# Softmax sums from chunks added on VectorE, split pairs by query halves, and TensorE's order as one script

## The chip, the cores and the metric

The kernel runs on one core of a Trainium2 chip. The metric is device microseconds of one execution. Before the change the median of three runs is 417.61 us (417.56 to 417.89). Besides, one execution was taken with the hardware profiler; views of that profile and its trace are what the text argues from. The engines are TensorE (PE, its weight loads PEld), VectorE (DVE), ScalarE (ACT), GpSimd (POOL) and SyncE (SP, which here only issues DMAs).

## The reference

Cosine attention over 8 batches of 12 heads, 448 tokens, head size 64, followed by a two-matrix layer with x * cos(x) between:

```
q_n = q / (norm(q) + 1e-06);  k_n = k / (norm(k) + 1e-06)
attn = softmax(q_n @ k_n.T / 0.1)            # over the keys
x = (attn @ v) as [3584, 768]                # 12 heads of 64 side by side
h = x @ w_in                                 # 768 -> 2048
out = (h * cos(h)) @ w_out                   # 2048 -> 768, float32
```

What matters for the change is the denominator of the softmax: for each query the sum over 448 keys of the exponentials.

## The kernel before

**Work.** Two heads make a pair; there are 48 pairs (g), three to a unit (u, 16 units), six to a batch. The 448 tokens are seven blocks of 64. Keys lie on partitions, so for a pair the exponentials are a half chunk PH (one block of keys: its two halves of queries on the two halves of the partitions, 448 columns for both heads) and three full chunks PX 1 to 3 (two key blocks on 128 partitions each; 448 queries for each of two heads, 896 columns, bf16). `scores` (L722) writes the four chunks: a matmul group of four 64x64 tiles, 224 columns for the half chunk (L740) and 448 for a full one (L732), and then an exponential on ACT (L747).

`attend` (L752) makes from them the value product and the sums, in one of four PSUM tiles of two banks each (AV, SC0, SC1, MP): bank 0 holds the product (64 dimensions of two heads on 128 partitions), bank 1 the sums. Its stages 0 and 1 take the half chunk (`rest` L763, or `row` L777 for the product alone), stage 2 the three full chunks (`av` L784, four tiles of 128 rows by 32 columns), with the sums behind it as matmuls whose weights are ones. For these there are several forms:

- Pairs whose sums go through a DMA ("not direct", 34 of 48). `sm` (L791) puts chunks 1 and 2 into rows of their own, four matmuls of 448 columns. In units 6 to 15 ("alone", 28 pairs) `sm2` (L807) follows with the half chunk and chunk 3 in matmuls of 224, 336 and 112 columns; in pairs 6 and 12 to 16 `sm1` (L799) with chunk 3 in four of 224, while the half chunk's sums come from `rest`. Product and sums are then copied out together, 128x896 floats, by DVE (L889) or, for even pairs after 18 that are not in "vector", by ACT (L886). `chain` (L923), once a unit: gather the sums by DMA into 128 partitions (three transfers, two in units 2 and 4), add the parts (L938), reciprocal (L941), write to DRAM (L942), broadcast back (L944), and POOL multiplies x = product * reciprocal (L948).
- "Direct" pairs 0 to 5 and 47: sums by `sm32` (L827, strided groups of 224) or `sm64` (L842), Ln and Exp(-x) on ACT (L896 to L912).
- "Quarters" or split pairs 7 to 11, 17 and 23, also direct: in `quarter` (L817) the key blocks on the two halves of the partitions go to different banks, value product of one beside the sums of the other, in two rounds of three groups of 448 columns (L823), with `rest` of two groups of 224 (L773) between. ACT takes the Ln over 448 sums (L910), then the Exp (L912); DVE copies the product (L915); POOL multiplies (L916).

After the six pairs of a batch, `m1` (L963) computes h: 96 matmuls of 128x128 by 448 columns (L956), ACT the sine (L985), DVE the product into gT (L987). The second matrix M2 is worked off in small steps between the pieces of attention: `m2_quarters` (L1036) makes steps of four 64x64 matmuls of 384 columns (L1054); an output tile takes 32 steps and both banks of MP, and is copied out by DVE (L1021).

**Order.** Each operation is entered with what it reads and writes. PE's order is the order of entry (from the first M1 on); `Program.play` sorts the other engines' operations by a model with due times, and waits are set from the dependencies. An operation with `lock=True` (all of POOL's, and few of DVE's) shares one slot with the others of that kind in this model. PE's order comes from `pair` (L1227) with shares of M2 from "grid", "given", "lead" and others in PLAN, and for pairs 19 to 22 and 25 to 46 from a written "script" that `play` (L1185) reads: `s19.1` is scores chunk 1 of pair 19, `a`, `b`, `c` are the stages of `attend`, `f4` is four steps of M2, `m3` is M1 of batch 3. The PSUM tile of each piece is chosen in turn (`touch` L1188).

**Beside it.** SP issues the loads of q and k, the transposes of later pairs (L698), gathers, broadcasts and outputs. POOL squares (L643) and scales (L681) q and k for later units, and issues the loads of v; DVE reduces the squares (L650).

Of the kernel before, what the change touches and what calls it, by code (L numbers as in the profile page):

```python
# [18 lines left out]
    "swapped": {},  # L19
    "early": {2: (3, 3), 4: (3, 3), 5: (3, 3), 6: (3, 3)},  # L20
    "vector": (32, 38),
    "alone": range(6, 16),
    "script": {19: """
        s19.0 f9 s19.1 s19.2 f9 s19.3 f3 a18 f4 b18 s20.0 c18 c19 s20.1 f2 a19 f2 b19 s20.2 f4 s20.3 f4 s21.0 a20 f4 s21.1 b20
        f4 s21.2 f6 s21.3 f6 o201 c20 m2 c21 a21 f4 s22.0 b21 f7 s22.1 f5 s22.2 s22.3 f11
        """, 25: """
        a24 s25.0 f3 s25.1 f2 b24 c24 s25.2 f4 s25.3 f5 s26.0 f3 s26.1 f4 s26.2 f3 s26.3 a25 f3 b25 s27.0 c25 c26 s27.1 f1 a26
        f2 b26 s27.2 f4 s27.3 f3 m3 c27 a27 f4 b27 s28.0 f4 s28.1 f4 s28.2 f4 s28.3 s29.0 f3 s29.1 f3 s29.2 f6 s29.3 f2 a28 f2
        b28 s30.0 c28 c29 s30.1 a29 f3 b29 f1 s30.2 f2 s30.3 f4 s31.0 f6 s31.1 s31.2 f5 s31.3 f7 a30 f4 b30 s32.0 c30 c31
        s32.1 f2 a31 f2 b31 s32.2 f7 s32.3 f5 s33.0 s33.1 f5 s33.2 f5 s33.3 f6 m4 c32 c33 a32 f4 b32 a33 f4 b33 s34.0 f8 s34.1  # L30
        f4 s34.2 s34.3 f2 s35.0 f4 a34 f4 b34 f2 s35.1 c34 s35.2 f5 s35.3 f11 s36.0 s36.1 f5 a35 f5 b35 s36.2 f6 c35 s36.3 f5
        s37.0 f5 s37.1 f6 s37.2 s37.3 f10 a36 f3 b36 f3 s38.0 c36 c37 s38.1 a37 f4 b37 s38.2 f4 s38.3 f8 s39.0 s39.1 a38 f4
        b38 f4 s39.2 f4 s39.3 f4 c38 m5 c39 a39 f4 b39 s40.0 f4 s40.1 f4 s40.2 f4 s40.3 s41.0 f5 s41.1 f4 s41.2 f5 s41.3 a40
        f2 b40 s42.0 c40 c41 s42.1 a41 f3 b41 f1 s42.2 f4 s42.3 f8 s43.0 s43.1 f4 s43.2 f3 s43.3 f7 a42 f2 b42 s44.0 c42 c43
        s44.1 f2 a43 f2 b43 s44.2 f9 s44.3 f3 s45.0 s45.1 f3 s45.2 f3 s45.3 f10 m6 c44 c45 a44 f4 b44 a45 f4 b45 s46.0 f8
        s46.1 f1 s46.2 f6 s46.3 f5
        """},
    "after": (0, 1, 2, 0, 1, 2, 0, 1),
# [5 lines left out]
    "last": ((0,), (1,), (2,)),  # L44
    "folded": (0, 1, 2, 3),
    "grid": {2: (16, 5, 6), 3: (11, 3, 4), 4: (8, 2, 3)},
# [4 lines left out]
    "second": 0,  # L51
# [5 lines left out]
    "mixed": (3, (3, 0, 1, 2, 0, 1, 2, 0), (2, 3, 4, 0, 1, 5)),  # L57
# [7 lines left out]
    "six": (0, 8, 4, 4),  # L65
    "cycle": {13: 3, 14: 3, 15: 3, 16: 3, 17: 3, 18: 3, 46: 3, 47: 3},
    "quarters": (7, 8, 9, 10, 11, 17, 23),
    "turns": {3: (3, 0, 1, 2, 0, 1, 2, 0)},
    "lastbank": 2,
    "end": (4, 3, 0),  # L70
    "parts": {3: (0, 1, 2, 3), 4: (0, 1, 3), 14: (0, 1, 3), 10: (0, 1, 3)},
# [5 lines left out]
    "given": {13: (0, 0, 3, 2), 16: (4, 0, 5, 2), 22:(1,2,5,6), 34: (12, 4, 5, 6), 46: (12, 4, 3, 4), 47: (2, 2, 5, 4)},  # L77
    "roots": (3, (14, 0), (10, 0)),
    "lead": {33: 5, 45: 6, 12: 13, 21: 13},
    "vloads": {3: [(4, "x6"), (5, "x6")], 4: [(6, "x11")], 5: [], 6: [(7, "x15"), (8, "x15")]},  # L80
    "behind": {2: 8, 3: 0, 4: 8},
    "direct": (0, 1, 2, 3, 4, 5, 7, 8, 9, 10, 11, 17, 23, 47),
}
# [335 lines left out]
def bass_cosine_attention__then__act_gcu_kernel(  # L419
# [28 lines left out]
    XS = [UP * S * (3 + i) + HQ * (i + 1) for i in range(2)]  # L448
    XW = XS[1] + UP * S
# [36 lines left out]
    sums = sbs("sums", 2, [128, 3 * SPR], F32)  # L486
# [6 lines left out]
    tail = sb("tail", [128, 32], BF16)  # L493
# [21 lines left out]
    xsv = [xu.ap()[:, x : x + UP * S].rearrange("p (g s) -> p g s", g=UP) for x in XS]  # L515
# [9 lines left out]
    TURN = (1, 2, 0, 1, 2, 0, 1, 0)  # L525
    AFTER = PLAN["after"]
# [5 lines left out]
    SH = S * 3 // 4  # L532
# [51 lines left out]
    for x in XS:  # L584
        dve(lambda e, x=x: e.memset(xu.ap()[:, x - HQ : x], 0.0), (), ["gap"], HQ)
    dve(lambda e: e.memset(tail.ap(), 0.0), (), ["tail"], 32)
    for n in range(2):
        dve(lambda e, n=n: e.memset(tail.ap()[BP * n : BP * n + BP, 16 * n : 16 * n + 16], 1.0), ["tail"], ["tail"], 16)
# [133 lines left out]
    def scores(g, c, bank=None):  # L722
        j, y = g % 2, g % NT
        name, ph = PHs[1 + (c + 1) % 2 if bank is None else bank]
# [11 lines left out]
        def half(e):  # L736
# [11 lines left out]
            keys, [("PX", j, c) if c else ("PH", g % 3)], 2 * n, "E", label="exp%d.%d" % (g, c))  # L748

    opened, held, turned = {}, {}, set(PLAN["swapped"])  # L750

    def attend(g, direct, stages=(0, 1, 2)):  # L752
# [6 lines left out]
        ws = slice(32, 96) if direct else slice(64, 128)  # L759

        folded, swapped, alone = g in PLAN["folded"], g in turned, not direct and u in PLAN["alone"]

# [541 lines left out]
    for g in range(TD, LT):  # L1304
        transposes(g)
# [85 lines left out]
```

## Time and profile before

| what | value |
|---|---|
| median of three runs | 417.61 us |
| span of the profiled execution, first to last instruction | 415.5 us; median less span 2.1 us |
| busy: PE, ACT, POOL, DVE | 406.5, 269.1, 242.9, 192.1 us |
| exponentials on ACT, 128x896 (L747) | 144, mean 918 to 923 ns |
| evacuation 128x896 on DVE (L889), on ACT (L886) | 22 of 1.09 us, 12 of 0.92 us |
| POOL: scale (L681), square (L643) | 48 and 44, mean 1.68 and 1.69 us |
| Ln of 448 sums (L910), of 224 (L896) | 0.54 us, 0.36 us |
| DVE copies of 448 columns (L915), of 384 (L1021) | 0.62 us, 0.55 us |

The span is what the profiler saw between the first and the last instruction; the time of a run is longer by what lies around it. "Busy" counts an engine's instructions; on PE the ends of overlapping matmuls are modelled, and so the time between the starts of two groups says more of a group's cost than its length.

### The profile page before, as it was taken

Reading aid. Unit: us, or ns where it says so; the run is one execution under the profiler, and the core shown is the slowest. Engines: PE = TensorE matmul, PEld = TensorE weight load, DVE = VectorE, ACT = ScalarE, POOL = GpSimd, SP = SyncE. Lnnn points to the kernel's source line nnn. Section 1 sums busy time; section 2 is a strip of 40 time slices with the busy share of each in tenths; the row PEclk is TensorE's granted clock in tenths of the full one; section 3 lists DMA queues with packets and bytes.
Section 4 is the critical chain, followed back from the end, with each engine's and each line's share of the span. In section 5 each row is a group of like instructions: output and inputs, shape, how many; then the busy total and the mean of one; then the engine's idle time right before and its main releaser. Section 6 shows DMA issues by size and latency. Waiting matters only on the chain.

```text
span 415.5 us, 13462 instructions
## 1 busy us (share of the span) xinstructions
PE 406.5 (98%) x6018; PEld 241.3 (58%) x6018; DVE 192.1 (46%) x257; ACT 269.1 (65%) x361; POOL 242.9 (58%) x193
## 2 busy tenths in 40 slices
PE   7799999999999999999999999999999999999997
PEld 3454556655556655665566556675566656655565
DVE  4564744455663257323753087321962254223421
ACT  4987578984888746977498567674588656603500
POOL 4999977889772575948964577536896200150000
PEclk9999999999999999999999999999999999999999
DMA  8999999979979997779955991989964900441023
GB/s 195 254 253 226 210 221 153 230 163 199 161 111 156 178 227 167 155 150 211 198 124 79 215 255 28 163 143 216 249 131 93 188 2 5 112 120 39 0 72 81
DMA packets 81553, 63.70 MB, mean 153 GB/s; under 512 B 46296, under 2 KB 76504, under 8 KB 81496
## 3 DMA queue, kind: packets, MB, share of 16 engines
q1 hardware_dynamic: 63288, 50.16, 56.7%
q0 software_dynamic: 18048, 12.59, 20.5%
q8 instruction: 47, 0.77, 0.8%
q10 hardware_dynamic: 160, 0.10, 0.1%
q14 instruction: 10, 0.08, 0.1%
HBM read 54.98 MB, written 11.13 MB: 159 GB/s over the span
## 4 chain that ended last, share of the span: by engine, by line
PE 92%; ACT 2%; POOL 2%; DMA 1%; DVE 1%; SPq 1%; issue 0%; ACTq 0%; POOLq 0%
PE MP L1054 28%; PE SC L956 20%; PE AV L956 10%; PE SC L732 5%; PE MP L956 4%; PE MP L1083 4%; PE AV L787 3%; PE SC L787 3%; PE SC L1083 3%; PE AV L823 2%; PE AV L732 2%; PE AV L773 1%; DMA raw<-in_q_dram 1%; POOL qks L681 1%; PE MP L838 1%; PE AV L1083 1%
## 5 line engine op out<-in xcount | busy, mean ns | idle before, releaser
L1054 PE MATMUL MP<-W,gT 64*64 64x384 bf16 x2816 | 141.1, 323 | 0.6 <-DVE qkT L719 0.4
L747 ACT ACTIVATE PX<-SC 128x896 bf16<-128x896 f32 x116 | 103.9, 918 | 12.2 <-PE SC L732 10.2
L1054 PEld LDWEIGHTS MP<-W,gT 64*64 64x64 bf16 x2816 | 85.0, 107 | 31.1 <-PE MP L1054 2.2
L956 PE MATMUL SC<-xT,W 128*128 128x448 bf16 x444 | 91.0, 353 | 0.0
L681 POOL TENSOR_TENSOR qks<-raw,rn 128x896 bf16<-128x896 f32 (+1 forms) x48 | 79.7, 1678 | 13.8 <-ACT rn L673 13.3
L643 POOL TENSOR_TENSOR sq<-raw 128x896 bf16<-128x896 f32 x44 | 73.5, 1690 | 12.9 <-DMA raw<-in_q_dram 9.1
L985 ACT ACTIVATE cosb<-SC,cst 128x896 f32<-128x896 f32 x37 | 37.2, 1007 | 61.5 <-PE SC L956 54.0
L948 POOL TENSOR_TENSOR xT<-xu,RB 128x448 bf16<-128x448 f32 x34 | 37.8, 1136 | 54.9 <-DMA RB<-scr 54.9
L956 PEld LDWEIGHTS SC<-xT,W 128*128 128x128 bf16 x444 | 43.1, 98 | 40.5 <-POOL xT L948 0.6
L1021 DVE COPY osb<-MP 128x384 f32<-128x384 f32 x50 | 25.9, 553 | 78.5 <-PE MP L1054 54.2
L987 DVE TENSOR_TENSOR gT<-SC,cosb 128x896 bf16<-128x896 f32 x37 | 40.3, 1090 | 39.4 <-ACT cosb L985 38.8
L650 DVE TENSOR_REDUCE n<-sq 128x14 f32<-128x896 bf16 (+2 forms) x49 | 51.1, 1058 | 9.4 <-ACT sq L641 4.9
L956 PE MATMUL AV<-xT,W 128*128 128x448 bf16 x240 | 52.3, 353 | 0.0
L732 PE MATMUL SC<-qkT 64*64 64x448 bf16 x464 | 41.6, 355 | 0.5 <-ACT PX L747 0.3
L956 PEld LDWEIGHTS AV<-xT,W 128*128 128x128 bf16 x240 | 23.3, 98 | 21.8 <-ACT xu L886 0.3
L985 ACT ACTIVATE cosb<-AV,cst 128x896 f32<-128x896 f32 x20 | 20.1, 1007 | 22.4 <-PE AV L956 18.1
L916 POOL TENSOR_TENSOR xT<-xu,RB 128x448 bf16<-128x448 f32 x8 | 9.1, 1137 | 36.6 <-ACT RB L912 36.6
L747 ACT ACTIVATE PX<-AV 128x896 bf16<-128x896 f32 x28 | 25.8, 923 | 6.0 <-PE AV L732 5.9
L987 DVE TENSOR_TENSOR gT<-AV,cosb 128x896 bf16<-128x896 f32 x20 | 21.8, 1088 | 13.7 <-ACT cosb L985 13.4
L617 POOL DMA_DIRECT2D va<-in_v_dram x32 | 21.9, 692 | 7.5 <-DMA raw<-in_q_dram 4.0
L747 ACT ACTIVATE PH<-SC 128x448 bf16<-128x448 f32 x37 | 20.3, 549 | 4.4 <-PE SC L740 3.9
L560 ACT ACT_TABLE_LOAD x17 | 21.8, 1283 | 1.0 <-PEq L1373 0.7
(110 smaller groups left out, 470.3 us busy)
## 6 DMA issues: line engine op xcount, KB each, us to landing
raw<-in_k_dram SPq DMA_DIRECT2D x48, 224.0 KB, 5.7
raw<-in_q_dram SPq DMA_DIRECT2D x48, 224.0 KB, 6.2
out_dram<-osb SPq DMA_DIRECT2D x54, 192.0 KB, 3.5
va<-in_v_dram POOLq DMA_DIRECT2D x32, 192.0 KB, 6.8
RB<-scr SPq DMA_DIRECT2D x18, 336.0 KB, 4.7
W<-in_moe_w_in_dram POOLq DMA_DIRECT2D x4, 768.0 KB, 15.8
W<-in_moe_w_out_dram POOLq DMA_DIRECT2D x4, 768.0 KB, 18.5
RB<-scr SPq DMA_DIRECT2D x6, 224.0 KB, 4.1
```

What stands on the lines that cost most here:

```text
L643: pool(lambda e, x=x, y=y: e.tensor_tensor(y, x, x, ALU.mult), src_, dst, 0.1 + n * 1.78e-3, label="sq%d.%d" % (u, p)).pad = LATE if u > 1 ...
L650: dve(lambda e, w=w: e.tensor_reduce(out=n2v[i][:, 2 * p : 2 * p + 2, w], in_=sqv[p][:, :, w, :], axis=mybir.AxisListType.X, op=ALU.add), ...
L681: f = lambda e, s0=s0, s1=s1: e.tensor_tensor(qksv[i][:, p, s0:s1].rearrange("p s h d -> p h s d"), rawv[i][:, h, s0:s1, :], bass.AP(rn[i] ...
L732: m = e.matmul(ph[BP * o : BP * o + BP, a, 0:S], t[r, c - 1 + (NT3 + 1) * o, 0:BP], t[r, :, BP : 2 * BP], start=True, stop=True)
L747: act(lambda e: e.activation(PHv[g % 3] if c == 0 else PXv[j][:, c - 1], ph[:, :, 0:n], ACT.Exp, scale=1.0 / TAU), keys, [("PX", j, c) if ...
L948: pool(lambda e, p=p: e.tensor_tensor(xTv[b % 2][:, UP * i + p, :], xuv[:, u % 3, p, :], RBv[i][:, p, :], ALU.mult), [("RB", i, p), ("xa", ...
L956: t = e.matmul(ph[:, a, 0:S], W1v[:, order[c], 128 * n : 128 * n + 128], xTv[b % 2][:, order[c], :], start=(c == 0), stop=(c == NKC - 1))
L985: act(lambda e, ph=ph, cz=cz: e.activation(cosv[cz], ph[:, :, 0:S], ACT.Sin, bias=cst.ap()[:, 0:1], scale=1.0), names(gi) + ["cst0"], [("c ...
L987: dve(lambda e, ph=ph, cz=cz, gi=gi: e.tensor_tensor(gTv[:, 2 * gi : 2 * gi + 2, S * (b % 2) : S * (b % 2) + S], ph[:, :, 0:S], cosv[cz], ...
L1021: dve(lambda e: e.tensor_copy(dst, po[:, 0:n]), name, [("osb", o, hf)], n, label="osb%d" % t)
L1054: r = e.matmul(POH[b][x : x + 64, 0:HW], gTv[k, y, col + x : col + x + 64], W2v[k, y, HW * b : HW * b + HW], start=(y == 0 and h == 0), st ...
L1083: r = e.matmul(po[:, 0 : w[1] - w[0]], gTv[:, y, col : col + 128], W2v[:, y, w[0] : w[1]], start=(y == 0), stop=(y == NF - 1))
```

## The change

**Folds.** After the exponential of chunk 2, DVE adds chunks 1 and 2 into a new tile FO (128x896, bf16). In 21 pairs ("folds" 2) it adds chunk 3 too, after that exponential. This is done for the 34 pairs that are not direct and for the seven split pairs (one fold each). The ones matmul takes FO: `sm2` is now the half chunk (four matmuls of 224 columns, by a new ones tile `half`), `sm` takes FO in four strided matmuls of 224, and `sm1` chunk 3, in pairs with one fold only. All 34 pairs are "alone" now. The sums stand once, in 224 columns of the bank, queries split by halves of the 64-blocks.

**Evacuation and chain.** The sums (224 columns) and the product (448) are copied out separately; ACT does it for pairs 20, 22, 28, 34, 36, 38 and 40, DVE for the other 27. The gather is one transfer and needs no addition; POOL's multiply reads the broadcast reciprocals in the order of the halves.

**Split pairs.** `run_phase` and `ends` replace `quarter`: bank b holds query half b, product in its first 224 columns, sums in the next; two rounds of five groups of 224 columns (three value groups, FO, chunk 3), and two of 224 for the half chunk. Ln and the copy of the product are done in two halves of 224 columns, the Exp at once.

**Order.** From pair 6 to the end PE's order is one script, in which each piece names its PSUM tile (`s19.1=2`); `pair` is left for pairs 0 to 5. The tables "grid", "given", "lead", "cycle" and others go; the M1 stages get turns, early parts and chunk orders in "m1".

```
-    "vector": (32, 38),
-    "alone": range(6, 16),
+    "vector": (24, 26, 30, 32, 42, 44, 46),
+    "fold": 1,
+    "folds": {6: 2, 12: 2, 16: 2, 18: 2, 20: 2, 21: 2, 25: 2, 26: 2, 30: 2, 32: 2, 33: 2, 35: 2, 36: 2, 37: 2, 38: 2,
+            39: 2, 40: 2, 42: 2, 44: 2, 45: 2, 46: 2},
...
+        s6.0=2 s6.1=1 f7 s6.2=2 f4 s6.3=1 f7 a6=0 s7.0=2 b6=0 s7.1=1 c6=0 s7.2=2 s7.3=1 f6 s8.0=2 f4 s8.1=1 f4 d7=0 a7=0
+        s8.2=2 c7=0 f8 s8.3=2 f8 s9.0=2 s9.1=1 f3 d8=0 a8=0 s9.2=2 c8=0 f3 s9.3=1 f7 s10.0=2 f1 s10.1=1 f2 d9=0 a9=0
...
+        b24=0 c24=0 s25.2=2 f4 s25.3=1 f8 s26.0=0 s26.1=2 f4 s26.2=1 f5 a25=2 s26.3=0 f2 b25=2 s27.0=1 c25=2 c26=0
...
     def scores(g, c, bank=None):
...
+        if 1 < c < 2 + folds(g) and (not direct(g) or g in PLAN["quarters"]):
+            x = PXv[j][:, 0].rearrange("p a s -> p (a s)") if c == 2 else FO[j].ap()
+            dve(lambda e: e.tensor_tensor(FO[j].ap(), x, PXv[j][:, c - 1].rearrange("p a s -> p (a s)"), ALU.add),
+                [("PX", j, c), ("PX", j, 1) if c == 2 else ("F", j)], [("F", j)], S, lock=True, label="fold%d" % g,
+                bias=PLAN["bf"][c - 2])
...
         def sm(e):
-            w = ones.ap()[:, 80:112] if alone else ones.ap()[:, 32:64]
             for n in range(2):
                 for a in range(2):
                     o = 64 * a + 32 * n
-                    t = e.matmul(av_[o : o + 32, 1, 0:S], w, PXv[j][:, n, a, :], start=alone or swapped, stop=False)
+                    t = e.matmul(av_[o : o + 32, 1, 0:SH], ones.ap()[:, 32:64], FOv[j][:, a, :, n, :], start=False, stop=folds(g) > 1)
             return t
...
-        def quarter(e, c, n):
...
+        def run_phase(h):
+            todo = [("V", c, ("PX", j, c + 1)) for c in range(NT3)] + [("F", 0, ("F", j))]
+            if folds(g) < 2:
+                todo.append(("S", 2, ("PX", j, 3)))
...
-                P.op("PE", sm, ["ones", ("PX", j, 1), ("PX", j, 2)], [ks], cost=MM, mode="C32", label="S%d" % g)
-                if alone:
-                    P.op("PE", sm2, ["ones", "tail", ("PH", g % 3), ("PX", j, 3)], [ks], cost=0.15, mode="C32", label="S%d" % g)
-                else:
+                P.op("PE", sm2, ["half", ("PH", g % 3)], [ks], cost=HALF, mode="C32", label="S%d" % g)
+                P.op("PE", sm, ["ones", ("F", j)], [ks], cost=HALF, mode="C32", label="S%d" % g)
+                if folds(g) < 2:
                     P.op("PE", sm1, ["ones", ("PX", j, 3)], [ks], cost=HALF, mode="C32", label="S%d" % g)
...
+        dma("SP", [lambda e: e.dma_start(sums[i].ap()[:, 0:w], bass.AP(xu, XS[i], [[32 * XW, 4], [w, 32], [1, w]]))],
...
+            dve(lambda e: e.reciprocal(r, x), [("sums", i)], ["rcp"], 8 * w, label="recip", bias=PLAN["rush"].get(u, 0.0))
```

More of the change, by code (lines that the diff above doesn't have):

```diff
@@ L723, in scores @@
         j, y = g % 2, g % NT
+        assert bank is None or bank not in holder
+        assert all(x > g - (3 if c == 0 else 2) for x in unfinished)
+        unfinished.add(g)
         name, ph = PHs[1 + (c + 1) % 2 if bank is None else bank]
@@ L1185, in play @@
     def play(text):
[L1186 to L1192 removed]
+        phase, made, finished = {}, {}, [PB]
         for w in text.split():
             kind, rest_ = w[0], w[1:]
[L1196 to L1198 removed]
             if kind == "f":
```

350 lines of the change are left out of this document (156 added, 194 removed), and 14 rows, old and new, of the table PLAN.

## The prediction

> **What bounds the kernel now.** I read the page first, for the share of each engine and the chain of work that ended last:
>
> ```profile
> PE 406.5 (98%) x6018; PEld 241.3 (58%) x6018; DVE 192.1 (46%) x257; ACT 269.1 (65%) x361; POOL 242.9 (58%) x193
> ...
> PEclk9999999999999999999999999999999999999999
> ...
> PE 92%; ACT 2%; POOL 2%; DMA 1%; DVE 1%; SPq 1%; issue 0%; ACTq 0%; POOLq 0%
> ```
>
> TensorE (PE) is busy for 98% of the span of 415.5 us, at full granted clock, and 92% of the chain lies on it. The busy share flatters it, since matmuls overlap, so I went on to the start times. In the list of waits PE itself waits some 5 us in all, nearly all before 62 us. From there to the end I added, for each matmul, the step from its start to the next start: of 350.1 us, 335 are columns streaming (0.417 ns each: a step of 0.189 for 448 columns less one of 0.0955 for 224), 5 are the few ns between groups, 7 are changes of tile shape (56 of them, about 0.12 us each), and 3 are stalls. So in all but the first 62 us a microsecond taken from PE's stream is a microsecond of time, unless another engine is as full. The stage table shows where one is (columns: stretch; busy of PE, PEld, DVE, ACT, POOL; clock; DMA share; GB/s):
>
> ```profile
> 57.30:89.40 32.10, 31.58 (x677) 19.50 (x670) 13.14 (x18) 28.91 (x45) 24.61 (x21) 1.00 0.98 195
> ...
> 161.00:187.00 26.00, 26.00 (x606) 17.45 (x606) 10.26 (x16) 21.88 (x32) 19.83 (x15) 1.00 0.66 139
> ...
> 248.70:282.00 33.30, 33.30 (x764) 23.10 (x766) 14.28 (x20) 23.71 (x32) 16.77 (x13) 1.00 0.65 115
> ...
> 302.00:327.70 25.70, 25.69 (x612) 17.50 (x612) 10.06 (x15) 22.72 (x32) 15.75 (x11) 1.00 0.62 125
> ```
>
> These are attention stages between two M1 stages. In the first, ScalarE (ACT) is busy 28.9 of 32.1 us, and after 67 us it hardly ever idles: there ACT is a second bound. In the later ones ACT is at 71 to 88%, VectorE (DVE) at about 40%, GpSimd (POOL) at 50 to 76%: PE alone is the bound.
>
> **What the sums cost PE.** The steps between starts in the timeline of PE (columns: start, length, instruction) give the price of each old form:
>
> ```profile
> 346.53 0.36 PE L796 MATMUL AV<-PX,ones 128*32 128x448 bf16 x4
> 346.72 0.31 PE L811 MATMUL AV<-PX,ones 128*32 128x336 bf16 x1
> ...
> 346.86 0.74 PE L787 MATMUL SC<-PX,va 128*32 128x448 bf16 x12
> ```
> ```profile
> 18.17 0.46 PE L831 MATMUL AV<-PX,ones 128*32 128x224 bf16 x12
> 18.56 0.38 PE L732 MATMUL SC<-qkT 64*64 64x448 bf16 x4
> ```
> ```profile
> 65.61 0.35 PE L823 MATMUL AV<-PX,ones 64*64 64x448 bf16 x2
> 65.62 0.35 PE L823 MATMUL AV<-PX,va 64*64 64x448 bf16 x2
> 65.80 0.35 PE L823 MATMUL AV<-PX,ones 64*64 64x448 bf16 x2
> ...
> 66.18 0.26 PE L773 MATMUL AV<-PH,ones 64*64 64x224 bf16 x2
> 66.19 0.26 PE L773 MATMUL AV<-PH,va 64*64 64x224 bf16 x2
> 66.28 0.36 PE L732 MATMUL SC<-qkT 64*64 64x448 bf16 x4
> ```
>
> The sums of a late pair run from 346.53 to 346.86, 0.33 us: 0.19 for a group of four matmuls of 448 columns and 0.14 for the mixed group. L831 has three groups of four of 224 columns, in the very form (128 rows by 32 columns, strided input) that the new sums take: 0.39 us with a shape change of 0.10, so 0.096 a group. In 64x64 tiles a group of 448 steps 0.19 (65.61 to 65.80), one of 224 steps 0.10 (66.18 to 66.28).
>
> *Taken from PE.* (a) The 28 pairs 18 to 46 without 23 pay 0.33 now. They will pay three groups, 0.29, in the 10 pairs with one fold, and two, 0.19, in the 18 with two: 10 x 0.04 + 18 x 0.14 = 2.9 us. (b) Pairs 6 and 12 to 16 pay 0.19 + 0.10 and half of their two opening groups (0.10): 0.38. They go to 0.19 (6, 12, 16) or 0.29 (13 to 15): 0.9 us. (c) The seven split pairs now run six groups of 448 and two of 224, 1.33 us; then twelve of 224, 1.15: 0.18 each, 1.3 us. Together 5.1 us, of which 1.1 (pairs 6 to 11) fall in the stage up to 89 us and **4.0 us** behind it.
>
> *Order.* I counted the new script: the visits to 128x32 tiles follow the same pairs as in the trace (shared by two pairs where they are now, as 28 with 29), so the shape changes stay at about 56. Between two output tiles of M2, whose two banks must first be copied out (2 x 0.55 us, L1021), the script leaves other matmuls of mostly 1.1 us or more. The pairs do not begin another M1 stage earlier or later. I count the order at 0; it could take back at most the 3 us of stalls, or cost about as much.
>
> *The stage up to 89 us.* There each split pair now costs ACT one Ln of 448 columns (0.54 us, L910) and then two of 224 (0.36 each, L896): 5 x 0.17 = +0.9 us for an engine with about 3 us idle in 32, most of it before 67 us. PE's 1.1 us can be kept only where ACT is not waited for. Ends: -1.1 and +0.9; I take **-0.4 us**.
>
> *Added on DVE: the folds.* 41 first and 21 second additions of 128x896 bf16. No row has such an instruction; the nearest:
>
> ```profile
> L987 DVE TENSOR_TENSOR gT<-SC,cosb 128x896 bf16<-128x896 f32 x37 | 40.3, 1090 | 39.4 <-ACT cosb L985 38.8
> ...
> L719 DVE COPY qkT<-MP 128x896 bf16<-128x896 bf16 x8 | 5.0, 622 | 3.7 <-PE MP L705 3.5
> ```
>
> A tensor-tensor with float input takes 1.09 us, a bf16 copy of that size 0.62. All operands of a fold are bf16, as the copy's are, so I take 0.62: 62 x 0.62 = 38 us (68 at the other end). [...] The evacuation adds five more pairs to DVE (27 where 22 were, in two copies of 0.62 and about 0.39 for 1.09): +3 us; the reduction of gathered sums (L938) goes: -2; split copies of (c): +1. DVE goes from 192 to about 233 us of some 412, still idle 40% of the time; ACT loses five of twelve evacuations of 0.92 us. None of it is on the path by its size. On SP the gathers drop from 34 issues (in the trace) to 13; the chain of sums was no bound (PE's loads waited 0.6 us for xT), so 0.
>
> *The wait that is added.* PE's sums now wait for a fold, which waits for the exponential. Behind the sums in PE's queue stands everything else. The path: matmul to ACT 0.22 (66.28 + 0.19 to 66.69), exponential 0.92, fold 0.62, two handovers: about 1.9 us. Against it stands the PE work that the script puts between the last scores that a fold needs and the sums (0.16 us a step of M2, 0.19 or 0.10 a score group, 0.57 the value product): 2.1 to 2.7 us in pairs 6, 16, 17, 26, 46; 2.8 to 3.2 in 7, 13, 14, 15, 37, 23 and 29; over 3.3 in the rest. So folds that start at once cost nothing. A fold held up by the POOL instruction in progress (if the two exclude each other) waits 0.47 us on average: that is half the squared lengths of POOL's 112 tensor instructions from 57 to 345 us over those 288 us. Drawn against each pair's cover this makes 1.6 us of PE stalls, nearly all in the five tight pairs. Ends 0 and 1.6; I take **+1.0 us**.
>
> **Sum.** -4.0 - 0.4 + 1.0 = -3.4 us. The profiled execution has a span of 415.5, and the median of the runs is 417.61, 2.1 more around it; I keep these 2.1: a span near 412.1 and **414.2 us**.
>
> **Rivals.**
> *Folds too late (slower).* DVE is in order: a fold may stand behind a reduction of 1.08 us (L650) and then be kept out by POOL, not for one instruction but for a whole run of them, which here last up to 15.9 us. The same sum as above gives, with 1 us more of path, 8.6 us of stalls: 417.6 - 4.4 + 8.6 = 421.8; with whole runs (1.86 us mean wait) some 33 us, 446. It decides from a mean stall of 4.4 / 41 = 0.11 us a pair. For it: POOL is 50 to 76% busy in these stages, and five pairs have under 0.8 us to spare. Against: the covers of the other pairs, and DVE's idle 40%. No contest of this kind is in the trace: DVE's one operation with two SBUF inputs (L681, 0.55 us) meets no POOL tensor instruction. [...] Chance 0.15.
> *Gain handed back (same).* PE's microseconds saved become waits for ACT's exponentials: in the stages at 84 to 88%, six pairs take 19.8 us of exponentials. For no gain, ACT would have to be at 100% after losing 1 us of PE in 26; it is not, but if folds stall 3 us more as well, the time is 417. Chance 0.09.
> *The whole saving arrives.* No stall, ACT absorbs the split Ln, and some of today's 3 us of stalls go: 417.6 - 5.1 - 1.2 = 411.3. Chance 0.2 beside the forecast's 0.56.
>
> **Numbers.** A measurement tells about 0.2% (0.8 us) from no change. Faster 0.56 + 0.2 = 0.76, same 0.09, slower 0.15. The range goes from 411.3 up into the mild half of the slow case, 418.8, and leaves out about 0.15.
>
> **What would show it.** Right: in the page after, PE still 98% and the chain over 90% PE; sums as groups of 224 with 0.096 between starts; folds of about 0.6 us; attention stages after 89 us shorter by 0.5 to 0.9 each, the first hardly. Wrong: PE or PEld waiting for DVE folds in the list of waits by more than 2 us; folds of over 1 us or stretched by POOL; DVE's multiplies of M1 late, and PE waiting for banks there; ACT idle less than 1 us in the first stage while it is longer than 32.1 us.

## The result and the profile after

The changed kernel takes 429.51 us (median of four runs, 428.33 to 431.7) beside 417.75 us of the kernel before on the same chip: ratio 1.028, 95% interval 1.0246 to 1.0314. The forecast was 414.2 and the range ended at 418.8: wrong in sign, by 15 us. The profiled execution after has a span of 426.5 us, 11.0 more than before. Its page, the shares of the engines, the granted clock and the shares of the chain:

```profile
PE 407.5 (96%) x6102; PEld 248.3 (58%) x6102; DVE 265.9 (62%) x344; ACT 263.2 (62%) x370; POOL 249.9 (59%) x192
...
PEclk9999999996899999999999999999999999999999
...
PE 90%; ACT 4%; issue 3%; DVE 2%; POOL 0%; POOLq 0%; DVEq 0%; ACTq 0%
```

PE's share fell from 98 to 96%, and the clock has a hole in two of the forty slices, at about 96 to 117 us. I took the start of the first and the last M1 matmul of each batch from the trace. That cuts the span into stages, and the loss stands in one of them (us; the last column is an experiment told below):

| stage | before | after | gap_all |
|---|---|---|---|
| attention up to the 2nd M1 stage | 31.67 | 31.54 | 32.71 |
| **2nd M1 stage** | **17.98** | **30.44** | **17.98** |
| next six attention stages | 39.18, 27.45, 25.82, 33.26, 25.86, 27.61 | 38.26, 27.43, 25.79, 32.87, 26.34, 27.11 | 38.26, 27.43, 25.79, 32.87, 26.33, 27.11 |
| all later M1 stages | 17.97 or 17.98 each | 17.97 or 17.98 each | 17.97 or 17.98 each |

So +12.46 in one M1 stage, and -1.5 in the seven attention stages together. The timeline of DVE, ACT and POOL at the start of that M1 stage (columns: start, length, instruction, how many merged):

```profile
89.14 0.85 DVE L754 TENSOR_TENSOR FO<-PX 128x896 bf16<-128x896 bf16 x1
...
89.46 1.34 POOL L617 DMA_DIRECT2D va<-in_v_dram  x2
...
90.03 14.43 DVE L754 TENSOR_TENSOR FO<-FO,PX 128x896 bf16<-128x896 bf16 x1
...
90.79 6.64 POOL L681 TENSOR_TENSOR qks<-raw,rn 128x896 bf16<-128x896 f32 x4
...
100.66 3.31 POOL L643 TENSOR_TENSOR sq<-raw 128x896 bf16<-128x896 f32 x2
...
104.38 1.08 DVE L1030 TENSOR_TENSOR gT<-SC,cosb 128x896 bf16<-128x896 f32 x1
```

The second fold of pair 12 (L754) takes 14.43 us where those that meet no POOL tensor work take 0.62. It ends 0.5 us after a run of eight POOL instructions (five scales and three squares, 90.79 to 103.97) has ended. Behind the fold in DVE's queue stands the first multiply of M1 (gT, L1030): it began at 104.38, with the fold's end, though the cosine that it needs had ended at 92.12. It frees the PSUM tile that M1's next matmuls need. The list of waits shows who paid (engine, line, releaser: us in total, times, longest):

```profile
ACT cosb L1028 <- DVE gT L1030: 23.6, 11, 13.5
...
PE SC L997 <- DVE gT L1030: 10.1, 1, 10.1
```

One wait of PE, 10.1 us, for DVE. Told by starts of matmuls, the step over this wait is 10.3 us longer than the others, and the twelve steps behind it lose 2.2 us to the clock: together the 12.46 us. The stretches of that time (columns: stretch; busy of PE, PEld, DVE, ACT, POOL; clock; DMA share; GB/s):

```profile
99.00:101.00 2.00, 0.00 (x0) 0.00 (x0) 2.00 (x1) 0.00 (x0) 2.00 (x3) 0.70 1.22 221
101.00:103.00 2.00, 0.00 (x0) 0.00 (x0) 2.00 (x1) 0.00 (x0) 2.00 (x2) 0.50 1.15 274
...
105.00:108.00 3.00, 2.40 (x7) 1.04 (x8) 1.93 (x3) 1.52 (x2) 0.26 (x1) 0.50 1.15 215
108.00:111.00 3.00, 3.00 (x12) 1.27 (x11) 1.61 (x2) 1.10 (x2) 0.00 (x0) 0.66 0.66 88
```

PE's last matmul before the wait has streamed at 95.3 us. After 4.5 us of idling, at 99.8, the clock granted to PE falls to 0.50, and it stays so to 110.0, for the first 4.4 us of work: matmuls of 448 columns then step 0.373 us instead of 0.189. In gap_late, below, it is 0.50 after a pause of 2.4 us.

### The profile page after: what moved, and what is told of

It reads as the page before. It is cut to its first block, busy times and chain, and to the rows that moved or that the text cites. A ratio compares the mean times of both kernels' runs of the same rounds, so it can differ in the third digit from the quotient of the medians.

```text
span 426.5 us, 13729 instructions
## 1 busy us (share of the span) xinstructions
PE 407.5 (96%) x6102; PEld 248.3 (58%) x6102; DVE 265.9 (62%) x344; ACT 263.2 (62%) x370; POOL 249.9 (59%) x192
## 4 chain that ended last, share of the span: by engine, by line
PE 90%; ACT 4%; issue 3%; DVE 2%; POOL 0%; POOLq 0%; DVEq 0%; ACTq 0%
PE MP L1097 26%; PE SC L997 21%; PE AV L997 9%; PE SC L735 6%; PE MP L997 4%; PE MP L1126 4%; PE AV L800 3%; PE SC L800 3%; PE SC L1126 3%; ACT PX L750 2%; PE MP L1156 2%; PE AV L835 2%; PE AV L735 1%; PE MP L868 1%; PE AV L1126 1%
## 5 line engine op out<-in xcount | busy, mean ns | idle before, releaser
L1097 PE MATMUL MP<-W,gT 64*64 64x384 bf16 x2816 | 137.2, 323 | 1.2 <-DVE osb L1064 0.6
L997 PE MATMUL SC<-xT,W 128*128 128x448 bf16 x468 | 97.1, 358 | 10.1 <-DVE gT L1030 10.1
L1097 PEld LDWEIGHTS MP<-W,gT 64*64 64x64 bf16 x2816 | 90.3, 107 | 26.5 <-PE MP L1097 2.6
L681 POOL TENSOR_TENSOR qks<-raw,rn 128x896 bf16<-128x896 f32 (+1 forms) x48 | 82.9, 1743 | 25.6 <-ACT rn L673 25.1
L986 POOL TENSOR_TENSOR xT<-xu,RB 128x448 bf16<-128x448 f32 x34 | 41.8, 1255 | 62.5 <-DMA RB<-scr 55.4
L997 PEld LDWEIGHTS SC<-xT,W 128*128 128x128 bf16 x468 | 46.0, 99 | 54.7 <-issue 14.1
L754 DVE TENSOR_TENSOR FO<-PX 128x896 bf16<-128x896 bf16 x41 | 47.1, 1148 | 37.0 <-ACT PX L750 36.7
L1030 DVE TENSOR_TENSOR gT<-SC,cosb 128x896 bf16<-128x896 f32 x39 | 42.4, 1088 | 32.8 <-ACT cosb L1028 32.4
L997 PE MATMUL AV<-xT,W 128*128 128x448 bf16 x216 | 45.6, 353 | 0.0
L754 DVE TENSOR_TENSOR FO<-FO,PX 128x896 bf16<-128x896 bf16 x21 | 31.3, 1489 | 3.5 <-ACT PX L750 2.5
L997 PEld LDWEIGHTS AV<-xT,W 128*128 128x128 bf16 x216 | 20.9, 98 | 19.7 <-DVE xu L933 0.3
L1030 DVE TENSOR_TENSOR gT<-AV,cosb 128x896 bf16<-128x896 f32 x18 | 19.6, 1087 | 10.8 <-ACT cosb L1028 10.8
```

Source lines behind the costliest of these rows:

```text
L681: f = lambda e, s0=s0, s1=s1: e.tensor_tensor(qksv[i][:, p, s0:s1].rearrange("p s h d -> p h s d"), rawv[i][:, h, s0:s1, :], bass.AP(rn[i] ...
L754: dve(lambda e: e.tensor_tensor(FO[j].ap(), x, PXv[j][:, c - 1].rearrange("p a s -> p (a s)"), ALU.add), [("PX", j, c), ("PX", j, 1) if c ...
L986: pool(lambda e, p=p: e.tensor_tensor(xTv[b % 2][:, UP * i + p, :].rearrange("p (s o m) -> p s o m", s=NB, o=2), xuv[:, u % 3, p, :].rearr ...
L997: t = e.matmul(ph[:, a, 0:S], W1v[:, order[c], 128 * n : 128 * n + 128], xTv[b % 2][:, order[c], :], start=(c == 0), stop=(c == NKC - 1))
L1030: dve(lambda e, ph=ph, cz=cz, gi=gi: e.tensor_tensor(gTv[:, 2 * gi : 2 * gi + 2, S * (b % 2) : S * (b % 2) + S], ph[:, :, 0:S], cosv[cz], ...
L1097: r = e.matmul(POH[b][x : x + 64, 0:HW], gTv[k, y, col + x : col + x + 64], W2v[k, y, HW * b : HW * b + HW], start=(y == 0 and h == 0), st ...
```

## The experiments

Two theories stood after this. **Shut out** (theory A in the expectations): folds and POOL's tensor instructions exclude each other, POOL keeps a fold out for a whole run of instructions, and one such fold is the loss. **Otherwise** (theory B): the folds' mere number, the new order or the new split pairs are the loss. All kernels ran beside the kernel before (417.6 to 417.9 us). PE's steps between starts, from 62 us on, are told as in the prediction: columns, shape changes, and the **rest**, which is stalls (3.0 us before, 18.9 after). A trace shows one run of a kernel; where that run lies far from the median, the text says so.

**1. port_order**: POOL's next planned tensor instruction waits for each fold.

```
+        taken = sorted((o for o in self.ops if o.eng == "POOL" and o.lock), key=lambda o: (o.start, o.idx))
+        for f in [o for o in self.ops if o.label.startswith("fold")]:
+            for o in [o for o in taken if o.start >= f.start][:1]:
+                o.deps.append((f, True))
```

> The changed kernel, with one thing added: after each fold the next GpSimd tensor instruction of the planned order waits for that fold, so that GpSimd cannot run on past a fold that is waiting for it. Theory A (folds are shut out by runs of GpSimd instructions, VectorE is in order, and the multiply of M1 stands behind the fold): the fold of 14.4 us shrinks below 2.4 us (the rest of one GpSimd instruction of 1.7 plus 0.62), the 10.1 us wait of TensorE and the half clock after it go, and the time is 414 to 417.5. Theory B (the new order, banks and early parts of the second M1 stage are too tight by themselves): the wait in that stage stays, 427 to 431.

418.37 us (416.22 to 419.98), ratio 1.0008 (0.9988 to 1.0028): 0.9 us above theory A's range and 8.6 below B's. The same place in its timeline:

```profile
90.93 1.34 POOL L621 DMA_DIRECT2D va<-in_v_dram  x2
...
91.49 0.62 DVE L758 TENSOR_TENSOR FO<-FO,PX 128x896 bf16<-128x896 bf16 x1
...
92.26 3.36 POOL L685 TENSOR_TENSOR qks<-raw,rn 128x896 bf16<-128x896 f32 x2
```

The same fold, with POOL's scale at the same distance behind its start (0.77 us), takes 0.62. The longest fold is 2.08 us. The 11 us are gone, all of them with the wait of M1. So the folds' order against POOL is the loss; 62 folds that get in cost about what they save.

**2. one_fold_12**: pair 12 has one fold instead of two; nothing else.

```
-    "folds": {6: 2, 12: 2, 16: 2, ...
+    "folds": {6: 2, 16: 2, ...
```

> The changed kernel with one fold in pair 12 in place of two: only the single fold that lasted 14.4 us is gone; its chunk is summed by TensorE (0.096 us more). Theory A: 12 us less, 416 to 418.5, as long as no other fold falls into that run of GpSimd instructions; folds elsewhere still held for up to 7 us. Theory B: no change, 428 to 431.

418.88 us (415.56 to 422.17), ratio 1.0008 (0.9981 to 1.0035), 0.4 us above A's range. Folds of 6.49 and 4.18 us remain in its trace (a run of 418.2) and cost little: from 62 us on PE's list has one wait for DVE of over 0.2 us, 0.4 us for a copy. A single instruction carried nearly all of the loss.

**3. no_folds**: chunks 1 and 2 go through the ones matmul as groups of their own, in the new order and the new split.

```
-    "fold": 1,
+    "fold": 0,
...
-                P.op("PE", sm, ["ones", ("F", j)], [ks], cost=HALF, mode="C32", label="S%d" % g)
+                for c in range(2):
+                    P.op("PE", lambda e, c=c: sm(e, c), ["ones", ("PX", j, c + 1)], [ks], cost=HALF, mode="C32", label="S%d" % g)
```

> The changed kernel with no fold at all: TensorE sums each chunk itself, in groups of 224 columns (15456 columns more than in the changed kernel, 6.4 us); order, banks, split pairs and evacuation as changed. Theory A: the stall of 12.5 us goes and so do most of the other new stalls (about 3 us): 429.5 - 15 + 6.4 = 421, between 418.5 (today's order was no worse than that of before) and 423.5. Theory B: 429.5 + 6.4 = 436.

423.41 us (421.8 to 427.26), ratio 1.0134 (1.0078 to 1.019), within A's range. Its trace is of the lowest of the four runs. Columns are 336.7 us against 330.4 with folds and 335.4 before; the rest is 5.9 us against 3.0 before. So the new order and split alone bring some 3 us of stalls or more, and folds that are not shut out pay: 5 us between this kernel and port_order.

**4. unread_folds**: as no_folds, but DVE makes the folds all the same and nobody reads them.

```
-        if 1 < c < 2 + folds(g) and (not direct(g) or g in PLAN["quarters"]):
+        if 1 < c < 2 + PLAN["idle"].get(g, 1) and (not direct(g) or g in PLAN["quarters"]):
...
```

> As the kernel without folds, but VectorE still does all 62 folds, whose result nothing reads. Theory A: the harm is VectorE standing still, not the sums waiting: a fold of over 10 us in the second M1 stage is back, and the time is 8 to 14 us above that of the kernel without folds. Theory C (the sums on TensorE wait for late folds, as the slower rival of the prediction had it): no sum waits for a fold here, so within 2 us of the kernel without folds.

427.3 us (423.57 to 428.6), ratio 1.0224 (1.0182 to 1.0266): 3.9 us above no_folds, outside what either theory had. Its trace has no fold of 10 us; one at 64 us took 4.5 us, kept out by two squares, and PE waited 2.1 us for DVE behind it. So the loss depends on where a fold falls against POOL's runs, and in this kernel it fell elsewhere. The trace is of the lowest of the four runs (423.57); what the higher ones lost isn't shown.

**5. before_fine.** In most kernels with new split pairs PE also paused where no wait stands. In port_order at 71 us (the last bracket is idle time and its releaser):

```profile
71.11 0.27 PE L848 MATMUL AV<-PH,va 64*64 64x224 bf16 x4
...
72.21 0.11 PEld L848 LDWEIGHTS AV<-PH,ones 64*64 64x64 bf16 x4 [1.07 <-issue]
```

I counted TensorE's instructions from the start: weight loads, matmuls and the waits between them. Between 62 and 90 us the pauses come when 1729, 1985, 2241 or 2497 of them have run, exactly 256 apart (854, 981, 1109 or 1236 weight loads). Each ends 1.3 to 1.7 us after a DMA of the kind "instruction" of 16384 bytes has landed; the traces have 47 to 50 of these DMAs, about one for each 256 instructions of TensorE. The DMA engines are 0.98 busy there (62 to 90 us, port_order). The new split runs more and smaller matmuls there (48 a pair against 32). The kernel before, with 448 columns cut in two of 224 in its split pairs, tests this without a fold:

```
-                    m = e.matmul(av_[64 * a : 64 * a + 64, k, 0:S], w, PXv[j][r, c, a, :],
...
+                    for h in range(2):
+                        x = slice(S // 2 * h, S // 2 * h + S // 2)
+                        m = e.matmul(av_[64 * a : 64 * a + 64, k, x], w, PXv[j][r, c, a, x],
...
```

> The kernel before, without any fold and in its own order; only the groups of 448 columns of the seven split pairs are cut into two of 224 each. Columns stay, 168 matmuls more (24 a pair), 120 of them between 62 and 90 us. In the kernels with the new split TensorE paused 0.5 to 1.35 us before a weight load that waits for no semaphore, each time 128 weight loads and 128 matmuls after the pause before it, up to 3.4 us in all in this stage. Theory (TensorE there runs through its instructions faster than they arrive): the pauses appear here too, 0.5 to 3 us in all between 62 and 90 us, and the median is 0.5 to 3 us above the kernel before. Rival (the pauses belong to the folds or to the new order): no pause over 0.3 us without a wait, and the time is within 0.5 us of the kernel before.

420.07 us (418.98 to 421.8), ratio 1.005 (1.003 to 1.0069). Pauses without a wait stand at 1729 and 2497, the same numbers, with steps of 0.36 and 0.41 us; the kernel before has no step over 0.3 us at these places. Another, of 0.66 us at 269 us, is of the same kind: it stands at 8641, 24 times 256 further on, 1.45 us after such a DMA. Together they are at most 1.4 of 2.5 us more rest; two waits for a transposed qkT (0.39 and 0.47 us, at 174 and 318 us) are a part of the others. So the finer matmuls do bring these pauses, in sizes of some tenths of a us; the median is 2.3 us above the kernel before, within the theory's range, but the pauses alone don't make it.

**6. old_split**: port_order with pairs 7 to 11 as in the kernel before.

```
+    "whole": (7, 8, 9, 10, 11),
...
+                    for c in range(NT3):
+                        P.op("PE", lambda e, c=c: quarter(e, c, 3 - n), [("va", y), ("PX", j, c + 1), "ones"], both_keys,
+                             cost=MM, mode="Q", label="AV%d" % g)
...
```

> As port_order (POOL's next planned instruction waits for each fold), but the five split pairs 7 to 11 in the form of the kernel before: six groups of 448 and two of 224, no fold; pairs 17 and 23 stay in the new form. Columns cost 0.9 us more, 80 matmuls fewer. Theory of the instruction supply: the pauses without a wait between 62 and 90 us, 2.0 us in port_order, fall below 0.5; 418.4 - 1.5 + 0.9, 417.0 to 418.2, and the runs scatter by less than 2 us (port_order: 3.8). Rival (the pauses come from the rest of the new order): they stay, and the time is 418.8 to 419.8.

420.65 us (418.35 to 425.23), ratio 1.0076 (1.004 to 1.0112). This is outside both ranges. In the profiled run the pauses shrank as forecast (0.39 us, from 2.0), the time did not: six of twelve runs lie at 418.4 to 419.7, one at 421.6 and five at 424.2 to 425.2. The profiled run is one of the low ones, so what the high ones do isn't in a trace. Nor does the old form always remove the pauses: the next two kernels that have it (experiments 8 and 10) pause 0.68 and 0.93 us at 1729.

**7. split_two**: port_order with a second fold in pairs 7 to 11.

```
-    "folds": {6: 2, 12: 2, ...
+    "folds": {6: 2, 7: 2, 8: 2, 9: 2, 10: 2, 11: 2, 12: 2, ...
```

> As port_order, but the split pairs 7 to 11 add chunk 3 on VectorE too: ten groups of 224 in place of twelve, 0.96 us fewer columns, 40 matmuls fewer, five folds more. Theory (with POOL held back folds cost little, and fewer instructions shorten the pauses): 416.5 to 417.8. Rival (more folds in the fullest stage hold up VectorE, POOL and so the exponentials): 418 to 420, with TensorE waiting for folds or for ACT between 62 and 90 us by over 1 us more than in port_order.

429.42 us (427.2 to 430.42), ratio 1.0265 (1.0237 to 1.0292), worse than the rival. The list of waits:

```profile
POOL xT L990 <- DVE FO L758: 21.3, 10, 9.0
...
PE AV L1001 <- POOL xT L990: 3.3, 1, 3.3
```

POOL's multiplies x = product * reciprocal now wait up to 9.0 us for a fold, and M1 waits for them. So a fixed order of POOL behind the folds can itself be a cost: port_order has the first of these rows at 20.5 us, only with hardly anybody waiting behind it. Whether it is what split_two lost is tested in experiment 11.

**8. old_split_turn**: old_split, with the two score tiles exchanged from `s19.1` on.

```
-... s19.0=2 f8 s19.1=2 s19.2=1 f10 s19.3=0 a18=2 f4 b18=2 f2
+... s19.0=2 f8 s19.1=1 s19.2=2 f10 s19.3=0 a18=1 f4 b18=1 f2
```

> As old_split, and from the second score chunk of pair 19 on the two score tiles change places in the script, so that this chunk no longer waits for the exponential of the chunk just before it (a TensorE wait of 0.57 us at 166 us in port_order). If that wait is on the path, 0.3 to 0.6 us less than old_split, 416.5 to 417.7; if the pieces behind it only wait in its place, the same as old_split.

419.6 us (418.61 to 424.63), ratio 1.0067 (1.0033 to 1.0101); the profiled spans are 417.1 and 416.5, and the rest from 140 to 200 us is 1.77 against 1.55. No gain shown: the second reading.

**What decides who gets in.** I then listed, in the traces so far, each case of a fold pending for more than 0.05 us when one POOL tensor instruction ended and the next stood right behind it. In runs of POOL that had begun after a gap the fold got in there, all 73 times. It was kept out, to the run's end, only in eight runs, and these had begun within 15 ns of the end of a DMA issue on POOL (the loads of v): at 90.8, 154.7 and 271.8 us in the changed kernel. A small edit can test such a rule.

**9. gap_all**: behind such a DMA issue POOL sets one element of a spare tile, and the next tensor instruction waits for that (twelve places).

```
+        queue = sorted((o for o in self.ops if o.eng == "POOL"), key=lambda o: (o.start, o.idx))
+        for y, o in zip(queue, queue[1:]):
+            if y.dma is not None and o.dma is None and o.start > 55.0:
+                t = self.op("POOL", self.pause, label="pause")
+                t.deps, t.start, t.end = [], o.start - 1e-6, o.start
+                o.deps.append((t, True))
...
+    P.pause = lambda e: e.memset(nil.ap()[0:1, :], 0.0)
```

> The changed kernel, with one small addition: behind each DMA issue on POOL, where a tensor instruction follows, POOL sets one element of a spare tile and the tensor instruction waits for that, so that no run of POOL's tensor instructions begins right behind a DMA issue. No fold waits for POOL's order or POOL for a fold. In the runs so far a fold that was pending when one POOL tensor instruction ended got in ahead of the next in every run of POOL that had begun after a gap, and was kept out to the end of the run in those that had begun without a gap behind a DMA issue. Theory (this decides): all folds get in at the first boundary, the longest is under 2.3 us, the 14.4 us one of pair 12 is gone and with it 12.5 us of the M1 stage: 416 to 418.5. Rival (the length of the run or the moment of the fold decides): folds of over 4 us stay, the time is within 3 us of 429.5.

**416.62 us** (415.7 to 421.25, eleven of twelve runs up to 418.36) beside 417.67 of the kernel before: ratio 0.998 (0.9956 to 1.0004); beside the changed kernel 12.9 us less. A gain over the kernel before isn't shown. Its timeline at the place:

```profile
90.73 1.34 POOL L625 DMA_DIRECT2D va<-in_v_dram  x2
...
91.29 0.62 DVE L762 TENSOR_TENSOR FO<-FO,PX 128x896 bf16<-128x896 bf16 x1
...
92.04 0.09 POOL L539 MEMSET nil<- 1x1 f32 x1
92.28 3.34 POOL L689 TENSOR_TENSOR qks<-raw,rn 128x896 bf16<-128x896 f32 x2
```

Twelve instructions of 0.09 us: the longest of the 62 folds is 2.07 us, all got in at the first boundary (but for one that had been pending for 0.03 us), and the second M1 stage is 17.98 us again. Here nobody waits for folds by order.

**10. gap_old_split**: gap_all with the split pairs 7 to 11 of old_split.

```
+    "whole": (7, 8, 9, 10, 11),
...
```

> As gap_all, and split pairs 7 to 11 in the form of the kernel before (448 columns, no fold), without the rule that POOL waits for folds. Columns 0.9 us more, 80 matmuls fewer. Theory (pauses for instructions between 62 and 90 us under 0.5 us, and old_split's runs of 424 us came from POOL's waits for folds): 416 to 418, scatter under 2.5 us. Rival (those runs have another cause): 418.4 to 425 again.

418.93 us (417.57 to 424.65), ratio 1.0032 (1.001 to 1.0053). Three of twelve runs are at 423.2 to 424.7 though POOL waits for no fold: the rival. The pause at 73 us (0.93 us) isn't under 0.5 either. What the runs of 424 do stays open.

**11. gap_split_two**: gap_all with a second fold in pairs 7 to 11.

```
+    "folds": {6: 2, 7: 2, 8: 2, 9: 2, 10: 2, 11: 2, 12: 2, ...
```

> As gap_all, and split pairs 7 to 11 add chunk 3 on VectorE too: 0.96 us fewer columns, 40 matmuls fewer, five folds more. Theory (split_two lost its 11 us because POOL's multiplies of the chain waited up to 9.0 us for folds that the rule put ahead of them, and M1 for them): without the rule 415.5 to 418. Rival (the five folds themselves are too much for the first stage): 419 or more, with TensorE waiting for folds there by more than 2 us.

427.42 us (425.41 to 428.4), ratio 1.0221 (1.0197 to 1.0244). So the rule of port_order was at most a small part of what split_two lost. No fold is over 2.05 us, but the rest from 62 us on is 16.5 us, spread over the stages: PE waits for a multiply of POOL (L994, 3.2 us once), for folds, and for copies. Here five more folds cost more than their columns save; which of these waits comes first isn't shown.

**12. reduce_folds**: a fold is one reduction over two chunks, so DVE reads one input from SBUF; one fold in each of the 41 pairs.

```
-            dve(lambda e: e.tensor_tensor(FO[j].ap(), x, PXv[j][:, c - 1].rearrange("p a s -> p (a s)"), ALU.add),
...
+            dve(lambda e: low(e, out=FO[j].ap(), in_=PXv[j][:, 0:2].rearrange("p c a s -> p (a s) c"),
+                                          axis=mybir.AxisListType.X, op=ALU.add),
...
```

> The changed kernel, with one fold in each of the 41 pairs, made by a VectorE reduction over the two chunks (one input from SBUF in place of two); 21 groups of 224 columns come back on TensorE, 2.0 us. By the reduction of 896 elements (1.08 us) one takes 1.9 to 2.0 us, and the sums wait 1.3 us longer. Theory (the two SBUF inputs make the contest): no reduction over 2.3 us, POOL's scale and square stay at 1.68 us with none at 2.07; the time is 419 to 422.5, with some 1 to 4 us of TensorE waits for folds. Rival (any VectorE work on SBUF beside POOL is held up): reductions of over 3 us, POOL stretched as before.

424.39 us (424.07 to 425.12), ratio 1.0159 (1.0144 to 1.0174), 2 us above the range. The groups, with POOL's scale (busy, mean ns of one, then idle before):

```profile
L758 DVE TENSOR_REDUCE FO<-PX 128x896 bf16<-128x1792 bf16 x41 | 82.7, 2018 | 30.0 <-ACT PX L749 29.8
L680 POOL TENSOR_TENSOR qks<-raw,rn 128x896 bf16<-128x896 f32 x47 | 78.6, 1691 | 13.9 <-ACT rn L672 13.3
```

All 41 take 2.006 to 2.022 us, beside the same POOL runs, and no scale is over 1.73 us. With two inputs a POOL instruction ahead of which a fold got in takes 2.07 instead of 1.68, or 1.52 instead of 1.14. This fits the two SBUF inputs as the cause of the contest. The runs don't separate it from what else differs between the two instructions: a reduction takes 2.02 us where an addition takes 0.62. The time is paid otherwise: 1.9 us of columns, 1.4 us more until the sums are there, and PE waits 1.9 us for copies of products and 0.8 for folds.

**13. gap_one**: of the twelve pauses only the one ahead of the run at pair 12. **14. gap_late**: all but the first two, at 64 and 88 us. The edit beside gap_all:

```
-        for y, o in zip(queue, queue[1:]):
-            if y.dma is not None and o.dma is None and o.start > 55.0:
+        places = [o for y, o in zip(queue, queue[1:]) if y.dma is not None and o.dma is None and o.start > 55.0]
+        for o in places[2:3]:        (gap_late: places[2:])
```

> The changed kernel with one pause only: POOL's memset of one element between its DMA issue and the run of eight tensor instructions that shut out pair 12's second fold for 14.4 us. Theory (that fold is the whole loss): this fold takes 0.62 us, the folds of 6.8 and 4.2 us later in the program stay and cost under 1 us; 429.5 - 12.5, so 416.3 to 418.5. Rival (the other folds that were shut out have their share): 419 or more.

> As gap_all, without the first two of its twelve pauses (at 64 and 88 us). Theory (the pause at 64 us shifts POOL's scaling and so a transpose, for which TensorE waited 1.3 us at 83 us): 0.5 to 1.3 us less than gap_all, 415.3 to 416.2. Rival (that wait is chance from run to run): as gap_all, 416.2 to 417.2.

gap_one 419.02 us (416.06 to 421.49), ratio 1.0021 (0.9994 to 1.0047); gap_late 420.12 us (415.9 to 421.96), ratio 1.0041 (1.0013 to 1.0068). Both have runs of 416 to 417.6 (five and three of twelve) and more of 418.6 to 422. By its median gap_one falls to its rival: more than one fold has a share. But its trace (a run of 416.86) shows which folds have none: those of 6.87 and 4.17 us are there, the second M1 stage is 17.98 us, and the span is 415.0 beside 415.2 in gap_all. And gap_late, which leaves only the first two places without a pause, is 3.5 us above gap_all, against both of its readings. Its profiled run, one of the higher (421.9), shows why (the last line is a stretch, with the columns as above):

```profile
62.96 1.41 POOL L626 DMA_DIRECT2D va<-in_v_dram  x2 [2.86 <-DVE xu L942]
63.49 4.70 DVE L763 TENSOR_TENSOR FO<-PX 128x896 bf16<-128x896 bf16 x1 [0.53 <-ACT PX L759]
...
64.38 3.33 POOL L652 TENSOR_TENSOR sq<-raw 128x896 bf16<-128x896 f32 x2
...
68.25 0.29 PE L844 MATMUL AV<-FO,ones 64*64 64x224 bf16 x4 [2.35 <-DVE FO L763]
...
68.50:71.90 3.40, 3.40 (x64) 2.49 (x56) 2.14 (x6) 2.10 (x4) 0.14 (x1) 0.50 0.54 69
```

The pause at 64 us, which I had taken for the cause of a late transpose, was keeping another fold from being shut out: here it takes 4.7 us, PE waits 2.4, and for 3.4 us the clock is 0.50. The wait for the transpose is there without that pause too (1.5 us). In the profiled runs of the changed kernel, one_fold_12 and gap_one the same fold, with POOL's square 0.88 us behind its start, took 0.62 or 0.63. So at this place it goes either way from run to run. One such stretch at half clock takes the mean clock of a run from 1.000 to 0.996. Runs with 0.995 or 0.996 are three of ten in one_fold_12, four of twelve in gap_one and six of twelve in gap_late, but one of twelve in gap_all and none of ten in port_order. That fits this fold as the cause of the scatter; shown in a trace it is only for the one run of gap_late, and in unread_folds (4.5 us).

## Why the prediction was wrong, point by point

**PE's columns: right.** The steps from 62 us on hold 330.4 us of columns after and 335.4 before, 4.9 less; the prediction had 5.1. Shape changes: 56, as counted.

**Length of a fold: right for a fold alone, and too small in sum.** The 27 folds that met no POOL tensor instruction took 0.614 to 0.626 us; 0.62 was taken. The other 35 met one, so the 62 took 78 us and not 38:

```profile
L754 DVE TENSOR_TENSOR FO<-PX 128x896 bf16<-128x896 bf16 x41 | 47.1, 1148 | 37.0 <-ACT PX L750 36.7
...
L754 DVE TENSOR_TENSOR FO<-FO,PX 128x896 bf16<-128x896 bf16 x21 | 31.3, 1489 | 3.5 <-ACT PX L750 2.5
```

Even in gap_all they take 61.5 us, and DVE is busy for 249.8 us, where about 233 were forecast. (The gathers before were 36 issues in the trace, not 34; their term was 0.)

**"The wait that is added", +1.0 us: the step that failed.** It drew a fold's delay from the one POOL instruction in progress (0.47 us on average) and set it against the cover of PE's sums alone. That the two exclude each other was an "if" that no run of before showed. Both halves were wrong. A fold can be kept out for a whole run of POOL: 14.4 us in pair 12, 6.8 and 4.2 us later. And who waited was not the sums: it was M1's multiply, next in DVE's own queue, and through it M1's PSUM tiles. The prediction listed what stands behind the sums in PE's queue, and not what stands behind the fold in DVE's. There was cover for one instruction and not for a run: a fold of 0.62 would have ended at 90.65, and the cosine that the multiply needs ended at 92.12, so 1.5 us of cover; the multiply began 12.3 us later than that, at 104.38. For +1.0 us the runs showed 12.46: 10.3 of PE's wait and 2.2 at half clock.

**The rival "Folds too late" (0.15) had the mechanism, not the place.** It named whole runs of POOL up to 15.9 us. But it spread them as a mean over 41 pairs' sums (421.8 to 446 us). What came was one event at one place and a time in that span's lower half. Its sentence "No contest of this kind is in the trace" was no evidence either way: no DVE operation of that kind had a POOL run beside it in the trace of before. The contest came (a POOL instruction behind a fold that got in took 2.07 us for 1.68; the reductions with one input took 2.01 to 2.02 beside POOL), but the earlier start did not decide it: the fold had started 0.77 us ahead of POOL's scale and needs 0.62, and was shut out.

**"Order: 0": a term of about 3 us.** It said that the order could cost about 3 us, and it did: no_folds has 2.9 us more stalls than before, with the new split pairs as well as the new order. With folds that get in (gap_all), the rest is 7.6 us against 3.0. Of these 4.6 us the trace shows 1.5 in a wait for a transposed qkT at 83 us, 0.9 in waits for exponentials at 114 and 166, 1.0 in M2 steps that wait for the copies of their tile (260, 268, 321 us), and 0.35 in a pause without a wait at 71; the rest is smaller. None of it is a wait of the sums for a fold: what the +1.0 was meant for was near nothing.

**Stage up to 89 us: taken -0.4.** It was -0.1 after and +1.0 in gap_all (ends: -1.1 and +0.9). The mechanism was another one: from 62 to 90 us ACT was busy for 23.5 of 28.0 us in gap_all (25.2 before), and PE stood there not for ACT but in the pauses without a wait, for a transpose and, in part of the runs, for the fold at 63.5 us.

**What would show it.** Attention stages shorter by 0.5 to 0.9 each: only two of six were (0.9 and 0.5), one grew by 0.5. Folds stretched by POOL, and "DVE's multiplies of M1 late, and PE waiting for banks there", stood in the list for wrong, and both came.

**Sum.** With the shut-out removed the kernel takes 416.62 us, within the range and 2.4 above the forecast. That it is within the range is no support for the sum: the saving in columns, 4.9 us, is real, but 4.6 of it goes into new stalls that stood in the sum at about nothing (span 415.2 against 415.5 before). In the profiled run of the changed kernel the 12.46 us of one fold are more than the whole loss of 11.0; in other runs the fold at 63.5 us may add to it.

What stays open: why a POOL run behind a DMA issue shuts a fold out (the rule is a count over these traces and the test by pauses, not a mechanism), why it does so only in some runs at 63.5 us, what the higher runs of gap_one and gap_late do beyond the one that is traced, where the 11 us of five more folds go, and what the runs of 424 us in the three kernels with old split pairs are.

## What to carry to other kernels

Before a DVE addition of two SBUF tiles is put beside GpSimd work, look up the longest unbroken run of GpSimd instructions at each of its places, and what stands behind it in DVE's own queue, not only who reads its result. One such instruction in 62 cost more than all 62 saved (12.46 us beside 6.3 of columns, 336.7 less 330.4); one element set on GpSimd behind its DMA issues (0.09 us, twelve places) took the cost away (416.62 us). The reductions with one input showed no contest (2.01 to 2.02 us, all 41), but left this kernel at 424.39 us. When a kernel is 98% one engine, count an order written anew as a cost of its own until the trace shows its stalls.

## What the runs showed of the hardware

- Eight runs of GpSimd tensor instructions that had begun within 15 ns of the end of a DMA issue on GpSimd kept a pending DVE addition out to their end (the longest addition 14.4 us, behind eight instructions); the runs that began after a gap let it in at the next instruction's end, in all 73 cases of the first traces and all 112 of the later ones with additions, and the GpSimd instruction behind it took 0.38 to 0.39 us longer (2.07 for 1.68). With one element set on GpSimd ahead of such runs (0.09 us, gap_all) the longest of 62 additions was 2.07 us. Of the folds that started 0.7 to 0.9 us ahead of such a run, with nothing to order the two, four were done in time and three were kept out.
- Between 62 and 90 us, where the DMA engines were 0.98 busy (port_order), TensorE paused 0.3 to 1.5 us without a wait after 1729, 1985, 2241 or 2497 of its instructions, 256 apart, and 1.3 to 1.7 us after a 16 KB instruction DMA landed. The kernel before has no step over 0.3 us at these counts; with its own matmuls cut finer (before_fine) it has two there, 0.36 and 0.41 us, and one of 0.66 us at 269 us.
- After 4.5 us without work (the changed kernel, 95.3 to 99.8 us) TensorE's granted clock was 0.50, for 4.4 us of the work that followed; after a pause of 2.4 us (gap_late) it was 0.50 for 3.4 us.
